# An attention and feed-forward kernel: a planner is told that one PSUM bank is one place

## The chip, the cores and the metric

The kernel runs on one core of a Trainium2 chip. The metric is the time of one execution on the device, in microseconds (us). Every time below is read from a timed run or from one profiled execution of the kernel before.

## What is computed

Attention with a threshold comes first, for 8 batches of 8 heads, 576 positions of width 64. Its output, laid out as 4608 tokens of 512, goes through a feed-forward layer of width 2048:

```python
scores = scale * np.matmul(q, k.transpose(0, 1, 3, 2))
thresh = np.max(scores, axis=-1, keepdims=True) - tau
scores = np.where(scores >= thresh, scores, -1000000000.0)
attn = softmax(scores)                  # written out with exp, sum and a 1e-9
x = np.matmul(attn, v)                  # 4608 tokens x 512 after a transpose
h = x @ w_in                            # 512 -> 2048
g = s * np.maximum(h, 0.0)**2 + b
out = g @ w_out                         # 2048 -> 512
```

## The kernel before

**Attention.** The work goes by visits: one visit is a pair of heads of one batch and half of its query rows. A visit has four or five tiles of 128 query rows by 576 keys. A tile's scores are made by TensorE into the PSUM tiles s0, s1 (early on also o): lines 352 and 341 in the early visits, line 363 (four matmuls, in split precision) and line 374 (the last 64 rows) later. VectorE takes the row's extreme (L395), ScalarE the exponential (L406), VectorE the threshold and sum (L409), GpSimd the division (L413). The weights are then transposed, in the first 8 visits by TensorE (L423, L425), later by VectorE and DMAs, and TensorE multiplies them by the values into the PSUM tile pv (L476).

**Feed-forward.** 256 tokens make a block, 18 blocks in all, and a block has 16 steps, one for each 128 columns of the inner width: 288 steps. A step is:
- its first products: 12 matmuls of 128x256 on TensorE (L599), into one half of the PSUM tile h. That tile is one bank of 512 columns, and even and odd steps take its two halves in turn (`k`, L590 and L593);
- its rectifier on ScalarE (L606), which reads that half, then a square (L607) and a rounded copy gh (L609), and a remainder gl on GpSimd (L610, in the last block on VectorE);
- its second products: twice three matmuls of 128x512 (L616), that take gh and gl as stationary operands and add to the PSUM tile o.

In the first and the last step of a block the first products are two pieces of six matmuls. Once, after the first block's steps, a matmul of line 563 writes the whole tile h.

**What sets the order.** Everything is recorded by `plan.add` with an engine, a cost, the function that emits it, a list of keys that it reads and one of keys that it writes, and a time `at` that serves as first rank. Keys are plain names: `plan.add` makes an operation depend on the last writer of what it reads, and on the last writer and all readers of what it writes. After that, `Plan.run` lays all operations out in time, many times over, forward and backward, under 18 settings, keeps the layout whose replay under four random delays is best by its own arithmetic, and emits the operations in that order. Each engine then runs its own instructions strictly in that order. The waits in the program do not come from the keys: the tile framework places them, from the tiles that the emitted instructions read and write and the order in which they were emitted. So the keys decide the order, and the order and the framework decide who waits.

Before the change, the keys of tile h are `h0` and `h1` for the halves, and `hs`, which only writers name. A step's first products write `h0` or `h1`, and `hs`; the rectifier reads `h0` or `h1` alone. Thus the plan keeps the first products of two steps in order, and lets a step's first products start while the rectifier of the step before is still to come. The early transposes of L425, which also use tile h in every other tile, write `h0` and `h1`.

Of the kernel before, what the change touches and what calls it, by code (L numbers as in the profile page):

```python
# [13 lines left out]
AF = mybir.ActivationFunctionType  # L14
# [160 lines left out]
def tile_attention_ffn(ctx: ExitStack, tc: tile.TileContext, qT, kT, v, tau, w_in, w_out, s, b, out):  # L175
    nc = tc.nc
# [55 lines left out]
    def pe(cost, fn, r, w, at):  # L232
        plan.add("PE", (cost, cost + 170), fn, r, w, at)
# [7 lines left out]
    def act(cost, fn, r, w, at):  # L241
        plan.add("ACT", cost, fn, r, w, at)
# [318 lines left out]

    def sums(at):
        pe(900, lambda: nc.tensor.matmul(bank["h"], ones.bitcast(F32), bias_t, start=True, stop=True), ["bias", "ones"],
           ["h0", "h1", "hs"], at)
        act((480, 620), lambda: nc.scalar.mul(out=bias_t, in_=bank["h"], mul=b_t), ["h0", "h1", "b"], ["bias"], at)

    def xhl():
        if "xhl" not in lazy:
            lazy["xhl"] = [sb(t, [P, NC, NB], F32R) for t in ("xh", "xl")]
        return lazy["xhl"]  # L570

    class Block:
# [16 lines left out]
        def step(self, f, at):  # L589
            k = count["step"] % 2  # L590
            count["step"] += 1
            n = (count["step"] - 1) % NG
            ps, g, hi, lo = bank["h"][:, k * NB:(k + 1) * NB], gb[k], gh[n], gl[n]  # L593

            def products(cs):
                xh, xl = xhl()
                for c in cs:
                    for i, (w, x) in enumerate(((wi[0][f], xh), (wi[0][f], xl), (wi[1][f], xh))):
                        nc.tensor.matmul(ps, w[:, c, :], x[:, c, :], start=(c == 0 and i == 0), stop=(c == NC - 1 and i == 2))  # L599
            if f in (0, NF - 1):  # L600
                for c in range(0, NC, 2):
                    pe(6 * 120.9, lambda c=c: products(range(c, c + 2)), [("xh", c // 2), ("xl", c // 2), (f"w{f}", "i")], [f"h{k}", "hs"], at)
            else:
                pe(3 * NC * 120.9, lambda: products(range(NC)), [(x, c) for x in ("xh", "xl") for c in range(2)] + [(f"w{f}", "i")],
                   [f"h{k}", "hs"], at)
            act((272, 383), lambda: nc.scalar.activation(out=g, in_=ps, func=AF.Relu), [f"h{k}"], [f"g{k}"], at)  # L606
            act((322, 417), lambda: nc.scalar.activation(out=g, in_=g, func=AF.Square), [f"g{k}"], [f"g{k}"], at)  # L607
            eng, do = (nc.vector, dve2) if self.last else (nc.gpsimd, pool)
            act((302, 405), lambda: nc.scalar.copy(out=hi, in_=g), [f"g{k}"], [f"gh{n}"], at)  # L609
            do((712, 740), lambda: eng.tensor_tensor(out=lo, in0=g, in1=hi.bitcast(F32), op=ALU.subtract),  # L610
               [f"g{k}", f"gh{n}"], [f"gl{n}"], at)

            def second(t):
                ts_ = slice(t * P, (t + 1) * P)
                for i, (a, w) in enumerate(((hi, wo[0][f]), (hi, wo[1][f]), (lo, wo[0][f]))):
                    nc.tensor.matmul(bank["o"][:, t, :], a[:, ts_], w, start=(f == 0 and i == 0),  # L616
                                     stop=(f == NF - 1 and i == 2))
            for t in range(2):
                pe(3 * 231.3, lambda t=t: second(t), [f"gh{n}", f"gl{n}", (f"w{f}", "o")],
                   [("o", t)] + (["o"] if f == 0 else []), at + SECOND)  # L620
# [115 lines left out]
    for f in range(FIRST_WEIGHTS):  # L736
        events.append((15 * f / FIRST_WEIGHTS, lambda f=f: convert(f)))
    step, when = 0, 0.0
    for i, (vs, j, t) in enumerate(tiles):
        joined = False  # L740
# [23 lines left out]
        for k_ in blocks:  # L764
            when = max(when, i + FFN_AFTER)
            each = 1.2 if i < 100 else 1.0

            def block(k_=k_, when=when, step=step, i=i, each=each):
                blk = make_block(*k_)
                blk.stage(max(i + FFN_AFTER, when - 1))  # L770
                for f in range(NF):
                    convert(f)
                    blk.step(f, when + each * f)
                    if not step and f == NF - 1:
                        sums(when + each * f + SUMS_AFTER)
                blk.finish(when + each * (NF + 1))

            events.append((i + (VALUES_AFTER if joins else 0) + 0.2, block))
            when += each * NF
            step += NF  # L780
# [47 lines left out]
```

## Time and profile before

| | us |
|---|---|
| timed runs, median of 3 | 1250.54 (1249.49 to 1253.12) |
| profiled execution, its own time | 1250.1 |
| profiled execution, first to last instruction | 1248.3 |
| TensorE busy in it | 1211.1 (97%) |
| ScalarE busy | 767.5 (61%) |
| VectorE busy | 807.1 (65%) |
| GpSimd busy | 719.7 (58%) |

Busy time is the union of an engine's instructions. TensorE's matmuls overlap one another in the records: one of 128x256 is shown for 0.28 us, and the next one starts 0.12 us after it, so idle time that the profile shows is a little less than what a pause really takes. In the rows, PE is TensorE, ACT ScalarE, DVE VectorE, POOL GpSimd, and L599 is line 599.

### The profile page before, as it was taken

To read this page: it belongs to the slowest core of one execution; us is meant where nothing else is said; L and a number is where in the kernel's file an instruction comes from. 1 tells how busy PE (TensorE), PEld (TensorE's weight loads), DVE (VectorE), ACT (ScalarE), POOL (GpSimd) and SP (SyncE) were. 2 spreads that over 40 slices of the span, in tenths; PEclk is the share of its full clock that TensorE was granted. 3 is DMA by queue.
4 is the path that set the end of the run, shared out by engine and by line. 5 is a ranking of instruction groups with operands and counts; after the bars stand their busy time and mean duration, and the time that the engine had idled before them with its cause. 6 is when DMAs were issued, how large, how long until landed. Compare 5 with 4: busy or idle time off the path is not lost.

```text
span 1248.3 us, 24523 instructions
## 1 busy us (share of the span) xinstructions
PE 1211.1 (97%) x7926; PEld 990.0 (79%) x7926; DVE 807.1 (65%) x2158; ACT 767.5 (61%) x1890; POOL 719.7 (58%) x822
## 2 busy tenths in 40 slices
PE   7789999999999999999999999999999999999998
PEld 5467778787887888788878888888888888887887
DVE  7987876667767676576666677666766666663011
ACT  5777755666666676565665666566656665653443
POOL 3766845576666775575565666557566656652200
PEclk7889999999999999999999999999999999999999
DMA  7950257678768776667666676566766666652000
GB/s 254 282 184 25 53 140 159 153 169 182 173 157 186 170 172 153 150 144 170 136 160 151 150 173 156 143 147 161 162 142 160 161 157 152 158 134 72 1 17 17
DMA packets 259534, 180.66 MB, mean 145 GB/s; under 512 B 83536, under 2 KB 238160, under 8 KB 259408
## 3 DMA queue, kind: packets, MB, share of 16 engines
q1 hardware_dynamic: 259120, 178.98, 59.0%
q8 instruction: 63, 1.03, 0.3%
q14 instruction: 63, 0.52, 0.1%
q10 hardware_dynamic: 288, 0.13, 0.0%
HBM read 87.03 MB, written 9.44 MB: 77 GB/s over the span
## 4 chain that ended last, share of the span: by engine, by line
PE 91%; DVE 4%; ACT 2%; issue 1%; DMA 1%; POOL 1%; SPq 0%; ACTq 0%; DVEq 0%; POOLq 0%
PE h L599 33%; PE o L616 32%; PE pv L476 12%; PE s L363 9%; PE s L352 2%; PE s L374 1%; DVE s L395 1%; ACT g L606 1%; PE pv L425 1%; DVE tr L409 1%; DMA qr<-in_q_dram 0%; DMA tau_t<-in_tau_dram 0%; DVE em L409 0%; DVE k L549 0%; PE o L352 0%
## 5 line engine op out<-in xcount | busy, mean ns | idle before, releaser
L599 PE MATMUL h<-xh,w 128*128 128x256 f32 x2304 | 466.7, 286 | 11.3 <-ACT g L606 11.0
L599 PEld LDWEIGHTS h<-xh,w 128*128 128x128 f32 x2304 | 376.9, 190 | 38.2 <-ACT g L606 23.5
L616 PE MATMUL o<-w,gh 128*128 128x512 f32 x1152 | 366.8, 400 | 0.8 <-DVE em L636 0.6
L599 PE MATMUL h<-xl,w 128*128 128x256 f32 x1152 | 326.1, 283 | 1.5 <-DVE xl L585 1.4
L610 POOL TENSOR_TENSOR gl<-g,gh 128x256 fp32r<-128x256 f32 x272 | 202.8, 747 | 212.0 <-ACT gh L609 188.2
L395 DVE TENSOR_SCALAR_CACHE_REDUCE s<-s,nsc 128x576 f32<-128x576 f32 x283 | 230.5, 819 | 143.1 <-PE s L363 120.8
L413 POOL TENSOR_SCALAR em<-em,st,zero 128x576 f32<-128x576 f32 x270 | 230.1, 853 | 156.7 <-DVE st L412 102.2
L409 DVE SCALAR_TENSOR_TENSOR em<-s,st,em 128x577 f32<-128x577 f32 x268 | 217.5, 812 | 105.8 <-ACT st L404 67.9
L406 ACT ACTIVATE em<-s,st 128x576 f32<-128x576 f32 x268 | 197.8, 738 | 95.9 <-DVE s L395 62.4
L616 PEld LDWEIGHTS o<-w,gh 128*128 128x128 f32 x1152 | 197.0, 189 | 46.3 <-issue 20.4
L616 PE MATMUL o<-w,gl 128*128 128x512 f32 x576 | 225.1, 391 | 0.0
L599 PEld LDWEIGHTS h<-xl,w 128*128 128x128 f32 x1152 | 219.7, 191 | 6.1 <-DVE xl L585 2.0
L446 DVE STREAM_TRANSPOSE tr<-em 128x512 f32<-128x512 f32 x252 | 178.2, 707 | 56.9 <-POOL em L413 47.3
L606 ACT ACTIVATE g<-h 128x256 f32<-128x256 f32 x288 | 109.2, 380 | 171.0 <-PE h L599 160.6
L328 POOL TENSOR_TENSOR k<-kr,k 64x576 fp32r<-64x576 f32 x104 | 148.5, 1428 | 54.1 <-ACT k L327 40.2
L476 PE MATMUL pv<-er,vb 128*64 128x256 f32 (+1 forms) x1280 | 172.8, 416 | 1.6 <-ACT er L434 1.6
L609 ACT CAST gh<-g 128x256 fp32r<-128x256 f32 x288 | 116.2, 405 | 56.6 <-PE o L616 52.9
L363 PE MATMUL s<-k 128*128 128x288 f32 x832 | 144.1, 297 | 0.6 <-POOL k L328 0.6
L363 PEld LDWEIGHTS s<-k 128*128 128x128 f32 x832 | 127.7, 188 | 19.7 <-issue 4.9
L476 PEld LDWEIGHTS pv<-er,vb 128*64 128x64 f32 x1280 | 86.4, 138 | 70.5 <-issue 12.9
L616 PEld LDWEIGHTS o<-w,gl 128*128 128x128 f32 x576 | 108.4, 188 | 24.5
L607 ACT ACTIVATE g<-g 128x256 f32<-128x256 f32 x288 | 119.9, 417 | 5.7
(104 smaller groups left out, 953.3 us busy)
## 6 DMA issues: line engine op xcount, KB each, us to landing
er<-tr SPq DMA_DIRECT2D x448, 160.0 KB, 3.3
kr<-in_k_dram SPq DMA_DIRECT2D x116, 288.0 KB, 4.2
vb<-in_v_dram SPq DMA_DIRECT2D x128, 128.0 KB, 2.8
qr<-in_q_dram SPq DMA_DIRECT2D x56, 160.0 KB, 4.4
er<-tr SPq DMA_DIRECT2D x112, 80.0 KB, 2.5
w<-in_moe_w_in_dram SPq DMA_DIRECT2D x16, 512.0 KB, 6.6
w<-in_moe_w_out_dram SPq DMA_DIRECT2D x16, 512.0 KB, 5.7
out_dram<-oo SPq DMA_DIRECT2D x30, 256.0 KB, 2.6
```

Source lines behind the costliest of these rows:

```text
L328: pool((1500, 1500), lambda: nc.gpsimd.tensor_tensor(out=z()[D:P], in0=kr[D:P, j], in1=z()[D:P].bitcast(F32), op=ALU.subtract), rk + [("z" ...
L363: nc.tensor.matmul(flat[sk][:, S0 + hf * HS:S0 + (hf + 1) * HS], lazy["q"][:, x, j, qc], lazy["k"][:, j, cs], start=(x == 0), stop=(x == 1))
L395: dve((740, 875), lambda: nc.vector.tensor_scalar(out=ps[:, S0:S0 + S], in0=ps[:, S0:S0 + S], scalar1=nsc, scalar2=None, op0=ALU.mult, op1 ...
L406: act((632, 740), lambda: nc.scalar.activation(out=ev, in_=ps[:, S0:S0 + S], func=AF.Exp, bias=st8[:, 0:1], scale=-1.0), [sk, (ks_, 0)], [ ...
L409: dve((742, 830), lambda: nc.vector.scalar_tensor_tensor(out=eb, in0=ps[:, S0:S0 + S + 1], scalar=st8[:, 1:2], in1=eb, op0=ALU.is_le, op1= ...
L413: pool((795, 825), lambda: nc.gpsimd.tensor_scalar(out=ev, in0=ev, scalar1=st8[:, 4:5], scalar2=zero, op0=ALU.mult, op1=ALU.add), [em_k, ( ...
L446: nc.vector.transpose(out=to[:, :, 0:NQ].rearrange("p m c q -> p m (c q)"), in_=ev[:, 0:M].rearrange("p (m r) -> p m r", m=4))
L476: nc.tensor.matmul(ps[j * D:(j + 1) * D, 0:32 * nb], vb[r, n, j, c], er[r, n, j, 0:nb, 32 * c:32 * c + 32], start=(c == 0), stop=(c == 4))
L599: nc.tensor.matmul(ps, w[:, c, :], x[:, c, :], start=(c == 0 and i == 0), stop=(c == NC - 1 and i == 2))
L606: act((272, 383), lambda: nc.scalar.activation(out=g, in_=ps, func=AF.Relu), [f"h{k}"], [f"g{k}"], at)
L610: do((712, 740), lambda: eng.tensor_tensor(out=lo, in0=g, in1=hi.bitcast(F32), op=ALU.subtract), [f"g{k}", f"gh{n}"], [f"gl{n}"], at)
L616: nc.tensor.matmul(bank["o"][:, t, :], a[:, ts_], w, start=(f == 0 and i == 0), stop=(f == NF - 1 and i == 2))
```

## The change

The key `hs` is dropped. First products and the matmul of L563 write `h0` and `h1` both, and the rectifier reads both. The plan therefore puts the first products of a step behind the rectifier of the step before. No instruction's work, shape or cost is altered; all of them are planned anew.

```diff
     def sums(at):
         pe(900, lambda: nc.tensor.matmul(bank["h"], ones.bitcast(F32), bias_t, start=True, stop=True), ["bias", "ones"],
-           ["h0", "h1", "hs"], at)
+           ["h0", "h1"], at)
...
                 for c in range(0, NC, 2):
-                    pe(6 * 120.9, lambda c=c: products(range(c, c + 2)), [("xh", c // 2), ("xl", c // 2), (f"w{f}", "i")], [f"h{k}", "hs"], at)
+                    pe(6 * 120.9, lambda c=c: products(range(c, c + 2)), [("xh", c // 2), ("xl", c // 2), (f"w{f}", "i")], ["h0", "h1"], at)
             else:
                 pe(3 * NC * 120.9, lambda: products(range(NC)), [(x, c) for x in ("xh", "xl") for c in range(2)] + [(f"w{f}", "i")],
-                   [f"h{k}", "hs"], at)
-            act((272, 383), lambda: nc.scalar.activation(out=g, in_=ps, func=AF.Relu), [f"h{k}"], [f"g{k}"], at)
+                   ["h0", "h1"], at)
+            act((272, 383), lambda: nc.scalar.activation(out=g, in_=ps, func=AF.Relu), ["h0", "h1"], [f"g{k}"], at)
```

The order moves nearly everywhere. Two places on TensorE and one on ScalarE follow. In the names, the number right after a w is the step within its block (w2 is step 2), xh and xl are the two parts of the tokens, gh and gl those of the step's result, and the last number is only the buffer's. What stands in brackets is whom an instruction waits for: Activation is ScalarE, Pool GpSimd.

TensorE before, eighth block, from the first products of step 2 to those of step 3:

```order
L599 MATMUL h_102<-xl_610,w2_359 128x256
L599 MATMUL h_102<-xh_609,w2_359 128x256
L599 MATMUL h_102<-xh_609,w3_427 128x256 [waits Activation_49]
L599 MATMUL h_102<-xl_610,w3_427 128x256
L599 MATMUL h_102<-xh_609,w3_427 128x256 x2
```

Step 3's products stand right behind step 2's, and their first matmul waits for ScalarE. TensorE after the change, the same place:

```order
L599 MATMUL h_102<-xl_597,w2_390 128x256
L599 MATMUL h_102<-xh_596,w2_390 128x256
L616 MATMUL o_100<-w15_1403,gh0_92 128x512 x2
L616 MATMUL o_100<-w15_1403,gl0_95 128x512
L363 MATMUL s0_98<-k_1514 128x288 [waits DVE_49,Pool_49]
L363 MATMUL s0_98<-k_1514 128x288 [waits Pool_49]
L363 MATMUL s0_98<-k_1514 128x288 x2
L599 MATMUL h_102<-xh_596,w3_440 128x256 [waits Activation_49]
L599 MATMUL h_102<-xl_597,w3_440 128x256
```

Three second products of the block before and the four score matmuls of a tile now stand between the two steps' products.

TensorE before, near the program's end, where attention is over: from the first products of step 1 of a block to those of step 2.

```order
L599 MATMUL h_102<-xl_610,w1_299 128x256
L599 MATMUL h_102<-xh_609,w1_299 128x256
L599 MATMUL h_102<-xh_609,w2_359 128x256 [waits Activation_49]
L599 MATMUL h_102<-xl_610,w2_359 128x256
L599 MATMUL h_102<-xh_609,w2_359 128x256 x2
```

Steps 1 and 2 adjoin here, and so do the products of steps 0 to 4 of this block. TensorE after, the same place:

```order
L599 MATMUL h_102<-xl_597,w1_297 128x256
L599 MATMUL h_102<-xh_596,w1_297 128x256
L616 MATMUL o_100<-w15_1403,gh0_92 128x512 [waits DVE_49]
L616 MATMUL o_100<-w15_1403,gh0_92 128x512
L616 MATMUL o_100<-w15_1403,gl0_95 128x512
L599 MATMUL h_102<-xh_596,w2_390 128x256 [waits Activation_49]
```

Three second products of the block before have come between; steps 2 and 3 still adjoin there.

ScalarE before, eighth block, the rectifiers of steps 0 to 2 (g0 and g1 are the two buffers that they write):

```order
L606 ACTIVATE g0_90<-h_102 128x256 [waits PE_49]
L607 ACTIVATE g0_90<-g0_90 128x256 [waits Activation_49]
L609 CAST gh1_93<-g0_90 128x256 [waits Activation_49]
L606 ACTIVATE g1_91<-h_102 128x256 [waits PE_49]
L406 ACTIVATE em0_77<-s0_98,st0_71 128x576 [waits DVE_49,Pool_49]
L607 ACTIVATE g1_91<-g1_91 128x256 [waits Activation_49]
L606 ACTIVATE g0_90<-h_102 128x256 [waits PE_49,Pool_49]
```

ScalarE after, the same place, the rectifiers of steps 0 and 1:

```order
L606 ACTIVATE g0_90<-h_102 128x256 [waits PE_49,Pool_49]
L404 ACTIVATE st4_75<-st4_75,tau8_67 128x1 [waits DVE_49]
L607 ACTIVATE g0_90<-g0_90 128x256 [waits Activation_49]
L406 ACTIVATE em0_77<-s0_98,st4_75 128x576 [waits Pool_49]
L609 CAST gh1_93<-g0_90 128x256 [waits PE_49,Activation_49]
L606 ACTIVATE g1_91<-h_102 128x256 [waits PE_49,Pool_49]
L607 ACTIVATE g1_91<-g1_91 128x256 [waits Activation_49]
L609 CAST gh2_94<-g1_91 128x256 [waits PE_49,Activation_49]
L406 ACTIVATE em1_78<-s1_99,st3_74 128x576 [waits DVE_49,Pool_49]
```

More of attention's work stands between the rectifiers than before, and an exponential can stand close ahead of one.

## Rows read from the trace of the kernel before

**Rows 1.** Page, busy time by engine, share of the span, instructions

```profile
PE 1211.1 (97%) x7926; PEld 990.0 (79%) x7926; DVE 807.1 (65%) x2158; ACT 767.5 (61%) x1890; POOL 719.7 (58%) x822
```

**Rows 2.** Page, the chain that ended last, by engine

```profile
PE 91%; DVE 4%; ACT 2%; issue 1%; DMA 1%; POOL 1%; SPq 0%; ACTq 0%; DVEq 0%; POOLq 0%
```

**Rows 3.** Stretches: length, busy (count) by engine, granted clock, DMA share, GB/s

```profile
0.00:70.00 70.00, 54.59 (x272) 34.48 (x272) 60.02 (x166) 46.28 (x93) 38.85 (x47) 0.80 0.83 262
70.00:160.00 90.00, 84.17 (x537) 63.52 (x538) 71.27 (x171) 65.30 (x163) 65.63 (x64) 0.98 0.27 78
...
300.00:500.00 200.00, 198.66 (x1351) 164.87 (x1352) 141.17 (x390) 130.91 (x324) 128.85 (x149) 1.00 0.74 170
...
1100.00:1150.00 50.00, 50.00 (x315) 39.46 (x314) 24.22 (x66) 25.30 (x64) 21.69 (x27) 1.00 0.43 101
1150.00:1248.30 98.30, 90.87 (x568) 80.64 (x567) 12.13 (x25) 39.26 (x98) 11.94 (x16) 0.99 0.06 17
```

**Rows 4.** TensorE's waits: who, for whom, us in total, times, longest

```profile
PE h L599 <- ACT g L606: 11.0, 21, 1.0
PE s L352 <- DVE em L409: 4.9, 3, 4.1
...
PE s L423 <- ACT er L432: 2.2, 1, 2.2
...
PE h L563 <- ACT g L606: 1.0, 1, 1.0
```

**Rows 5.** Time line of TensorE, eighth block: start, length, [idle before, releaser]

```profile
571.00 0.28 PE L599 MATMUL h<-xh,w 128*128 128x256 f32 x1
571.75 0.38 PE L599 MATMUL h<-xh,w 128*128 128x256 f32 x1 [0.47 <-ACT g L606]
571.97 0.28 PE L599 MATMUL h<-xl,w 128*128 128x256 f32 x1
572.09 0.40 PE L599 MATMUL h<-xh,w 128*128 128x256 f32 x2
```

**Rows 6.** Time line of ScalarE at the same place

```profile
568.66 0.68 ACT L327 CAST k<-kr 128x576 fp32r<-128x576 f32 x1 [0.23 <-DMA kr<-in_k_dram]
571.31 0.38 ACT L606 ACTIVATE g<-h 128x256 f32<-128x256 f32 x1 [1.98 <-PE h L599]
```

**Rows 7.** Time line of TensorE, first and last of 15 adjoining steps that paused

```profile
80.40 0.39 PE L599 MATMUL h<-xh,w 128*128 128x256 f32 x1 [0.47 <-ACT g L606]
1206.51 0.39 PE L599 MATMUL h<-xh,w 128*128 128x256 f32 x1 [0.47 <-ACT g L606]
```

**Rows 8.** Time line of TensorE, pauses at steps with other work between

```profile
118.38 0.39 PE L599 MATMUL h<-xh,w 128*128 128x256 f32 x1 [0.62 <-ACT g L606]
234.15 0.39 PE L599 MATMUL h<-xh,w 128*128 128x256 f32 x1 [0.54 <-ACT g L606]
302.92 0.39 PE L599 MATMUL h<-xh,w 128*128 128x256 f32 x1 [1.05 <-ACT g L606]
770.38 0.38 PE L599 MATMUL h<-xh,w 128*128 128x256 f32 x1 [0.16 <-ACT g L606]
901.47 0.39 PE L599 MATMUL h<-xh,w 128*128 128x256 f32 x1 [0.76 <-ACT g L606]
```

**Rows 9.** Time line of TensorE: second products, and scores, between two steps' products

```profile
575.44 0.70 PE L363 MATMUL s<-k 128*128 128x288 f32 x4
576.13 0.39 PE L599 MATMUL h<-xh,w 128*128 128x256 f32 x1
...
1226.21 0.63 PE L616 MATMUL o<-w,gh 128*128 128x512 f32 x2
1226.68 0.39 PE L616 MATMUL o<-w,gl 128*128 128x512 f32 x1
1226.91 0.62 PE L616 MATMUL o<-w,gh 128*128 128x512 f32 x2
...
1227.60 0.28 PE L599 MATMUL h<-xh,w 128*128 128x256 f32 x1
```

**Rows 10.** ScalarE's costliest lines: busy, mean ns, idle before and its releasers

```profile
L406 ACT ACTIVATE em<-s,st 128x576 f32<-128x576 f32 x268 | 197.8, 738 | 95.9 <-DVE s L395 62.4 <-DVE st L412 17.3 <-POOL gl L610 7.2
...
L606 ACT ACTIVATE g<-h 128x256 f32<-128x256 f32 x288 | 109.2, 380 | 171.0 <-PE h L599 160.6 <-POOL gl L610 6.6 <-POOL k L331 1.8
```

**Rows 11.** Stretch at the start, columns as in rows 3

```profile
10.00:20.00 10.00, 9.29 (x30) 5.78 (x31) 8.88 (x28) 5.83 (x12) 2.61 (x4) 0.55 0.96 329
```

## Prediction

> **What bounds the kernel now.** I read the page's busy times first. TensorE is busy 1211.1 of 1248.3 us, the next engine, VectorE, 807.1 [rows 1]. The chain of waits says the same: 91% of what ended last is TensorE's own work [rows 2]. So time can only be won where TensorE stands idle, 37.2 us in all, and the table by stretches tells where: 15.4 us in the first 70 us, 5.8 in the next 90, 1.3 in the 200 us from 300 to 500, none from 1100 to 1150, 7.4 in the last 98.3, most of which lies behind TensorE's last matmul [rows 3]. The list of waits names the causes. The largest by far is that first products (L599) wait for a rectifier (L606): 11.0 us in 21 pauses, and L563 waits once more for a rectifier, 1.0 us [rows 4]. Of the 21, 15 stand where a step's products follow the step before directly, each 0.47 to 0.53 us, 7.7 us in all, of which the first and the last are shown [rows 7]; the other six, 3.3 us, have other work between, and five of them are shown [rows 8].
>
> **How a pause at adjoining steps comes about.** The time lines at 571 us show it. The last product of a step starts at 571.00 and is shown for 0.28. ScalarE has been free since 569.34 (568.66 + 0.68), yet the rectifier starts only at 571.31, released by products [rows 6]; and it is the rectifier of the step before that, whose products had ended when this step's began. It waited for the other half of the bank to be written out. The next products start at 571.75 [rows 5], 0.06 after the rectifier's end. So in the program that runs, the two halves already exclude each other, and in the order in which they were emitted: where the plan emits a step's products before the last rectifier, that rectifier is held for a whole step, and the third step in a row pays the pause. The change takes no overlap away, since there is none; it tells the plan of a wait that is there anyway.
>
> A pause costs more than its idle time. From 571.97 to 572.09 one product follows the other after 0.12 us, though each is shown for 0.28 [rows 5]; so each pause costs its idle time and 0.16 more. At 571.75 that is 0.75 − 0.12 = 0.63; where the idle is 0.53 it is 0.69.
>
> **What the bank costs before.**
> - 15 pauses at adjoining steps: 7.7 + 15 × 0.16 = 10.1 us.
> - six with work between: 3.3 + 6 × 0.16 = 4.3.
> - L563: 1.0 + 0.16 = 1.2.
>
> Together 15.6 us, which is the most that the change can win here.
>
> **What it costs after.** I counted the 287 seams between the first products of neighbouring steps in both orders, and weighed the matmuls in each seam by start-to-start times: four score matmuls fill 576.13 − 575.44 − 0.16 = 0.53 us, six second products 1227.60 − 1226.21 = 1.39, so three fill 0.70 [rows 9]. Before, 63 seams put the products ahead of the last rectifier, 39 of them with nothing between; the other 224 are in the proper order, 17 of them with less than 0.8 us of work. After, all 287 are in the proper order; 2 have nothing between, 11 have under 0.8 us, 85 have 0.8 to 1.4, 189 more.
> - Two bare seams: at most 0.69 each, 1.4 us.
> - 11 short ones: the 17 of before had pauses of 0.54, 1.05, 0.16 and 0.76 [rows 8], with 4 × 0.16 that is 3.15, 0.185 per seam; so 2.0 us. (Bounds: 0, as at 13 of the 17, and 1.2 for each, 13 us.)
> - 274 with more: the 207 of before had two pauses, 0.62 [rows 8] and one that makes up the view's 11.0 with the rest, 0.16; with 0.32 that is 1.1, 0.005 per seam; so 1.5 us.
> - L563: in the new order three second products and four score matmuls stand between the step's last products and it: 0.
>
> Together 4.9 us; the gain is 15.6 − 4.9 = 10.7.
>
> What fills the seams is no new work, and it was somewhere before: does its cover now lack elsewhere? The second products of a step stand behind a chain of rectifier, square, copy and remainder. The nearest that they follow their first products in either order is 2.5 us of TensorE work at one place after and 4.2 before; in all other places it is over 4.1, as before. The score banks s0 and s1 are written again after as much work as before (4.1 us or more, at one place 3.4). ScalarE, GpSimd and VectorE have 35 to 42% to spare [rows 1]. I take 0 for this, within −1 and +2.
>
> **A rule that speaks against it.** At one seam, the rows show 0.75 us from the last product to the next one, the rectifier lying open in it [rows 5, 6]. The Trainium skill, Perfetto Trace Analysis, section Optimizing Tensor Performance (Matmuls), wants the opposite of one bank held in turn: independent groups of matmuls should rotate through PSUM banks, so that the emptying of one lies beside the next group's matmuls. By that rule alone, every seam would lie open, and the sum would be 287 × 0.69 = 198 us of loss in place of 4.9. The rows of before speak against it in this kernel: between two steps there is work for the banks o, s0, s1 and pv, and where 0.8 us or more of it stood there, 2 of 207 seams paused.
>
> **The start.** All operations are planned anew, the first 160 us too, where TensorE is idle 21.2 us [rows 3] and VectorE is busy 60.0 of 70. Ahead of the first products both orders have the same ten groups of scores, 17 groups of transposes and four value products; ahead of the eleventh step's, 15 groups of scores before and 16 after. I take 0. Bounds: the longest single waits there are 4.1 and 2.2 us [rows 4]; and the granted clock is 0.55 from 10 to 20 us [rows 11], close to the lower level (1.2 GHz, 0.5), so ten busy microseconds more or less of it are worth 4.5. Of these I take ±6 as the reach.
>
> **The sum.** The profiled execution took 1250.1 us, 1.8 more than its span. 1250.1 − 10.7 = 1239.4. The median of the timed runs is 0.4 above that execution, so 1239.8: I predict 1240.
>
> **The rivals.**
> 1. The start gives it back. If one more chain of 4.1 + 2.2 us lies open there and ten microseconds more fall to the lower clock, that is 6.3 + 4.5 = 10.8 against 10.7: 1250.6. For it: the start is where most idle time is, VectorE has no slack there, and this part of the plan moved as well. Against: the same work stands ahead of the first steps. Chance 0.16 (from +7 us on, it ends within 0.3%).
> 2. Slower: the rectifier is late. It runs in ScalarE's order, and behind an exponential of 0.74 us [rows 10] the least gap, 0.75 − 0.16 = 0.59 us, grows to 1.33; the 85 seams with 0.8 to 1.4 us between are then too thin. If they cost what the short ones do, 85 × 0.185 = 15.7 more, and the sum is 1239.8 + 15.7 = 1255.5. It turns the gain to nothing from 10.7 / 85 = 0.13 us a seam, and to slower from (10.7 + 3.8) / 85 = 0.17. For it: ScalarE is 61% busy, and there are more thin seams now. Against: of 45 such seams before none paused as long as the list of waits counts (0.15 us). Chance 0.06.
> 3. The skill's rule in full: 1239.8 + 193 = 1433, with all seams open. Chance 0.01.
> 4. The start wins too: 4 to 6 us of its idle time go along with the seams: 1235. Chance 0.07.
>
> **How the numbers follow.** The forecast has 0.70. About 0.3%, 3.8 us, is what a measurement of this kernel can tell from no change. Forecast and rival 4 are faster by more than that: 0.77. Rival 1 is the same: 0.16. Rivals 2 and 3 are slower: 0.07. The range: all of 15.6 won gives 1235, with a part of the start 1234; upwards it takes most of rival 1, up to 1248.
>
> **What would show it.** In the changed kernel's list of waits, L599 behind L606 should fall from 11.0 us in 21 pauses to 3 or 4 in under 10, and L563 should be gone. No adjoining pauses of 0.47 to 0.53 but at most two, late in the program. TensorE's idle time from 300 to 1150 us should be all but gone. ScalarE's idle time ahead of L606 (171.0 us [rows 10]) should fall, since no rectifier is held through another step's products. I am wrong if L599 still waits 8 us or more for L606, if pauses stand at seams with 0.8 to 1.4 us of work (rival 2), or if the idle time of the first 160 us moves by more than 6 from 21.2 (rivals 1 and 4).

## The result and the profile after

The changed kernel takes 1237.28 us, the median of 4 runs (1236.05 to 1237.95), against 1250.01 for the kernel before in the same runs: a ratio of 0.990, with a 95% interval of 0.987 to 0.992. Run again beside the experiments with pairs, it took 1237.42 (0.9888, 0.9865 to 0.9911). The forecast was 1240. The profiled execution took 1237.66 us and its span is 1235.7, 12.6 shorter.

TensorE's list of waits in the changed kernel (who, for whom, us in total, times, longest) begins thus:

```profile
PE s L352 <- DVE em L409: 3.6, 3, 2.7
PE s L423 <- ACT em L406: 3.0, 2, 2.3
PE pv L476 <- ACT er L434: 2.7, 3, 0.9
PE s L423 <- DVE s L395: 2.6, 1, 2.6
PE s L352 <- ACT er L432: 2.3, 1, 2.3
PE h L599 <- DVE xl L585: 2.0, 1, 2.0
...
PE h L599 <- ACT g L606: 1.0, 2, 0.5
```

First products waited 11.0 us in 21 pauses for a rectifier [rows 4]; now it is 1.0 in 2, and L563 is gone from the list. What leads it now is the early attention tiles' waits, of the first 160 us. The two pauses are at the two bare seams (nothing stands between two steps' products) of the new order:

```profile
1143.79 0.38 PE L599 MATMUL h<-xh,w 128*128 128x256 f32 x1 [0.53 <-ACT g L606]
...
1191.09 0.38 PE L599 MATMUL h<-xh,w 128*128 128x256 f32 x1 [0.47 <-ACT g L606]
```

How a filled seam looks, in TensorE's time line of the changed kernel, between two steps of the eighth block:

```profile
566.58 0.28 PE L599 MATMUL h<-xh,w 128*128 128x256 f32 x1
566.70 0.70 PE L363 MATMUL s<-k 128*128 128x288 f32 x4
567.23 0.63 PE L616 MATMUL o<-w,gh 128*128 128x512 f32 x2
567.70 0.39 PE L616 MATMUL o<-w,gl 128*128 128x512 f32 x1
567.93 0.28 PE L599 MATMUL h<-xh,w 128*128 128x256 f32 x1
```

and ScalarE beside it, the rectifier of the step that ended at 566.86:

```profile
566.96 0.38 ACT L606 ACTIVATE g<-h 128x256 f32<-128x256 f32 x1 [1.02 <-PE h L599]
```

It is done at 567.34, 0.6 us before the next products, and TensorE has no idle time in between. At the place of [rows 5] the rectifier came one step late and TensorE stood still for 0.47.

The stretches of the changed kernel (length, busy time and count by engine, granted clock, DMA share, GB/s):

```profile
0.00:70.00 70.00, 49.77 (x267) 31.33 (x267) 56.92 (x156) 45.08 (x90) 38.52 (x47) 0.85 0.77 252
70.00:160.00 90.00, 84.43 (x531) 63.88 (x529) 70.41 (x177) 65.56 (x162) 57.53 (x60) 0.94 0.29 85
...
300.00:500.00 200.00, 200.00 (x1359) 167.00 (x1359) 145.01 (x398) 131.17 (x328) 132.53 (x154) 1.00 0.74 172
```

Two things stand here beside [rows 3]. TensorE is idle 25.8 us of the first 160, where it was 21.2: 4.6 more. And from 300 to 500 us it is never idle, and 1359 matmuls run where it was 1351. The same view over 160 to 1150 us, of the kernel before and then of the changed one:

```profile
160.00:1150.00 990.00, 981.45 (x6554) 811.40 (x6553) 663.72 (x1799) 616.64 (x1538) 603.29 (x696) 1.00 0.66 155
```

```profile
160.00:1150.00 990.00, 988.02 (x6633) 822.80 (x6634) 661.76 (x1803) 621.91 (x1556) 608.22 (x704) 1.00 0.67 156
```

TensorE's busy time rises by 6.6 us, but 79 more matmuls run in the stretch, and at 990 / 6633 = 0.15 us each these are worth some 11.8, by an estimate that takes all matmuls for alike. The count in a fixed stretch shows what the idle time hides.

### The profile page after: what moved, and what is told of

The parts are those of the page before. It is cut to its first block, busy times and chain, and to the rows that moved or that the text cites. A ratio compares the mean times of both kernels' runs of the same rounds, so it can differ in the third digit from the quotient of the medians.

```text
span 1235.7 us, 24583 instructions
## 1 busy us (share of the span) xinstructions
PE 1202.7 (97%) x7926; PEld 989.8 (80%) x7926; DVE 800.5 (65%) x2158; ACT 766.2 (62%) x1890; POOL 713.1 (58%) x822
## 4 chain that ended last, share of the span: by engine, by line
PE 93%; DVE 3%; ACT 2%; issue 1%; DMA 1%; SPq 0%; POOL 0%; DVEq 0%; ACTq 0%; POOLq 0%
PE h L599 33%; PE o L616 33%; PE pv L476 13%; PE s L363 9%; PE s L352 2%; PE s L374 1%; DVE s L395 1%; PE pv L425 1%; DMA tau_t<-in_tau_dram 0%; PE s L341 0%; DMA er<-tr 0%; DVE tr L409 0%; PE s L423 0%; DVE em L409 0%; ACT em L406 0%
## 5 line engine op out<-in xcount | busy, mean ns | idle before, releaser
L599 PE MATMUL h<-xh,w 128*128 128x256 f32 x2304 | 469.3, 285 | 1.1 <-ACT g L606 1.0
L599 PEld LDWEIGHTS h<-xh,w 128*128 128x128 f32 x2304 | 378.8, 190 | 29.6 <-issue 8.5
L599 PE MATMUL h<-xl,w 128*128 128x256 f32 x1152 | 325.7, 283 | 2.0 <-DVE xl L585 2.0
L599 PEld LDWEIGHTS h<-xl,w 128*128 128x128 f32 x1152 | 219.5, 191 | 8.1 <-DVE xl L585 2.2
L606 ACT ACTIVATE g<-h 128x256 f32<-128x256 f32 x288 | 110.1, 382 | 183.9 <-PE h L599 167.4
```

## The experiments

The theory: the time is won at the seams, where a plan that knows of the bank's wait fills it. The first rival: any new plan moves the time by as much, and this one was lucky.

**Other settings of the planner, with the old keys and with the new.** `SHARES` and `LATER` are factors on the spare time that the planner adds to each operation, early in the program and later on. One of these lines differs, in two ways; each goes once with the keys of before and once with those of after.

```diff
-    SHARES = 0.2, 0.4, 0.7
+    SHARES = 0.25, 0.5, 0.8
```

```diff
-    LATER = 1.0, 1.2, 1.4
+    LATER = 1.1, 1.3, 1.5
```

> The keys of before, but the planner tries other settings (shares 0.25, 0.5, 0.8), so that everything is planned anew. In this order 43 seams between the first products of two steps have nothing between and 70 seams put the products ahead of the last rectifier (39 and 63 in the kernel before). Theory (the gain comes from the keys of the bank): 1250, within 4, with L599 waiting 9 to 14 us for L606. Rival (any new plan moves the time by 10 us or more, and this change was lucky): anywhere from 1235 to 1265, with no tie to the pauses at L599.

> The keys of after with the same other settings (shares 0.25, 0.5, 0.8). 4 seams with nothing between, none with the products ahead. Theory: 1238, within 4, at least 8 below its partner with the old keys; L599 waits under 4 us for L606. Rival (luck): it may lie anywhere, and not below its partner.

> The keys of before, a third set of settings (later 1.1, 1.3, 1.5). 43 bare seams, 69 with the products ahead. Theory: 1250, within 4, L599 waits 9 to 14 us for L606. Rival (luck): anywhere from 1235 to 1265.

> The keys of after with the third set of settings (later 1.1, 1.3, 1.5). 3 bare seams, none with the products ahead. Theory: 1238, within 4, at least 8 below its partner with the old keys; L599 waits under 4 us for L606. Rival (luck): not below its partner.

The ratios are to the kernel before as it ran beside each of them (medians 1250.01, 1251.28 for the pairs, 1248.96 for the wider search).

| kernel | median us | ratio to before | L599 waits for L606 | matmuls, 160 to 1150 us | TensorE idle, first 160 us | matmuls, first 160 us |
|---|---|---|---|---|---|---|
| before | 1250.01 | 1 | 11.0 us, 21 | 6554 | 21.2 | 809 |
| old keys, other shares | 1257.54 | 1.0059 (1.0039 to 1.0080) | 14.3, 29 | 6518 | 25.6 | 802 |
| old keys, other later | 1255.43 | 1.0035 (1.0017 to 1.0052) | 12.2, 24 | 6517 | 25.6 | 827 |
| after | 1237.28 | 0.9896 (0.9872 to 0.9920) | 1.0, 2 | 6633 | 25.8 | 795 |
| new keys, other shares | 1231.03 | 0.9844 (0.9814 to 0.9875) | 2.6, 5 | 6640 | 19.9 | 830 |
| new keys, other later | 1234.16 | 0.9868 (0.9843 to 0.9894) | 2.1, 5 | 6641 | 26.4 | 815 |
| wider search (below) | 1235.06 | 0.9887 (0.9860 to 0.9915) | 0.5, 1 | 6648 | 26.0 | 785 |

The pairs differ by 26.5 and 21.3 us, more than by 12.7. In the main part 6517 to 6554 matmuls run with the old keys and 6633 to 6648 with the new ones: in three plans against four the two groups lie far apart, so the keys decide that, not the plan's luck. The start goes by luck, as far as these plans show: 785 to 830 matmuls in the first 160 us, with no tie to the keys. Its idle time alone is a poor measure, since it also hangs on the granted clock. Two executions whose orders are the same in the start, of the changed kernel once more and of the one with bare pairs (both below), show it:

```profile
0.00:160.00 160.00, 133.97 (x795) 95.16 (x795) 127.25 (x332) 110.63 (x252) 96.12 (x106) 0.90 0.51 158
0.00:160.00 160.00, 137.93 (x798) 97.85 (x799) 128.00 (x334) 111.10 (x253) 94.77 (x107) 0.87 0.50 158
```

The second is idle 4.0 us less at a granted clock of 0.87 in place of 0.90, with only three matmuls more. By the counts, the kernel before had no lucky start among those of the old keys (809 beside 802 and 827); it was ahead of the other two in the main part, with 6554 matmuls and fewer pauses. The changed kernel, with 795, is the third of the four with the new keys. The forecast for the pairs missed on the size: the old keys came out 3.5 and 1.4 us above the range of 1246 to 1254, one of them with 14.3 us of waits where 9 to 14 were expected, and the new keys with other shares, at 1231.03, below 1234 to 1242; that is the best version found.

**The old order, with the rectifiers first.** The plan and its keys are those of before; only when operations are emitted, what a step's first products are put behind includes the last rectifier (and what that depends on).

```diff
-        return [ops[n][3] for _, n in self.order]
+        return [ops[n][3] for n in rectifiers_first(self)]
...
+def rectifiers_first(plan):
...
+        for d in sorted(plan.ops[n][4]) + [plan.ahead.get(n)]:
+            put(d)
```

> The plan of before, with its keys, but when the operations are emitted, each rectifier is put ahead of the next step's first products, with what it depends on. No rectifier is then held through another step's products, and the order of the matmuls stays nearly as it was: 30 seams have nothing between, 21 under 0.6 us. Theory (what costs is a seam that TensorE can't fill; the order on TensorE is what was won): 30 bare seams at 0.69 us are 20.7, against 10.1 before, and the short ones cost 3 to 5: slower than before by 5 to 12, 1255 to 1262, with L599 waiting 16 to 22 us for L606. Rival (what costs is the rectifier held in ScalarE's order, and what stands behind it): faster than before by 5 or more, 1245 or less.

Measured: 1286.2 us, 1.030 (1.027 to 1.032). The direction is the theory's and the rival is out, but the loss is 37 us where 5 to 12 were expected: L599 waits 39.2 us in 52 pauses. Of the 30 bare seams 27 pause for 0.47 to 0.53, as foretold. Of the other 22 pauses eleven take 1.49 to 1.88 us, most of these at seams that hold 1.39 us of second products. TensorE, ScalarE and GpSimd at one of them, in time lines of this kernel:

```profile
386.91 0.63 PE L616 MATMUL o<-w,gh 128*128 128x512 f32 x2
...
388.27 0.40 ACT L609 CAST gh<-g 128x256 fp32r<-128x256 f32 x1 [2.50 <-PE o L616]
388.76 0.72 POOL L610 TENSOR_TENSOR gl<-g,gh 128x256 fp32r<-128x256 f32 x1 [6.02 <-ACT gh L609]
...
389.51 0.38 ACT L606 ACTIVATE g<-h 128x256 f32<-128x256 f32 x1 [0.84 <-POOL gl L610]
...
389.95 0.39 PE L599 MATMUL h<-xh,w 128*128 128x256 f32 x1 [1.49 <-ACT g L606]
```

The rounded copy waits for a gh buffer, of which there are three, that second products have yet to read; GpSimd waits for the copy, the rectifier for GpSimd and its g buffer, and the next products for the rectifier. Where first products run ahead of second ones, the rectifier is at the end of that chain, and putting it first brings the whole chain in front of TensorE.

**Pairs with bare seams, and the same with held rectifiers.** These ask for the price of one seam with nothing else moved. Near the end of the changed kernel, 12 pairs of steps lose the second products between their first products, which follow behind the pair. In the second version the order on every engine is the same again, but the pair's first rectifier is emitted behind the pair.

```diff
+    for m in range(262, 286, 2):
...
+            if n in plan.second:
+                ahead[n] = last
```

```diff
+        rect = a + 1 + (plan.ops[a + 1][0] == "PE")
+        for n in range(b, last + 1):
+            plan.ops[n][4].discard(rect)
+        ahead[rect] = last
```

> The changed kernel once more, on the same chip as the two that follow. All theories: 1237, within 2.

> The changed kernel, but near the end, where attention is over, the first products of steps 262 and 263, 264 and 265, and so on to 284 and 285 are emitted without the second products between them, which follow behind the pair. Each rectifier still comes ahead of the next products. All matmuls stay, and the order on the other engines is the same; 13 seams are bare in place of 2. Theory (a bare seam costs 0.69 us on TensorE, a filled one nothing): 11 times 0.69 is 7.6, so 1244 to 1246, and L599 waits for L606 in 13 pauses or so, 6.5 us. Rival (the seams are not what the time hangs on, the plan as a whole is): 1237, within 2.

> The same order on every engine as in bare_pairs, but in each of the 12 pairs the first step's rectifier is emitted behind the second step's products, as the plan of before did it: TensorE need not wait inside a pair, and the rectifier is held until the second products of the bank are out. Theory (a held rectifier costs TensorE nothing as long as no third step follows at once; what costs is the wait for it): the 7.6 us go away again, 1237 to 1239. Rival (a rectifier that is held through another step's products costs time by itself, in ScalarE's order): 1242 or more.

Measured: 1237.42, 1245.95 (0.9967, 0.9955 to 0.9979) and 1237.15 (0.9897, 0.9877 to 0.9916), all three as the theory had them. With bare seams the kernel takes 8.5 us more, 0.78 for each of the 11; L599 waits 7.2 us in 14 pauses. One of the pairs, TensorE with bare seams:

```profile
1165.41 0.28 PE L599 MATMUL h<-xh,w 128*128 128x256 f32 x1
1166.22 0.38 PE L599 MATMUL h<-xh,w 128*128 128x256 f32 x1 [0.53 <-ACT g L606]
1166.44 0.28 PE L599 MATMUL h<-xl,w 128*128 128x256 f32 x1
```

From start to start that is 0.81 us in place of 0.12, and the second product, too, comes 0.22 after the first in place of 0.12. Together such a seam loses 0.79 us, and 0.73 where the idle time is 0.47. Six of the 11 new seams are of the first kind and five of the second: 8.4 us. Two other waits came with the new order. At a seam with three second products the next products wait 0.60 us, and elsewhere second products wait 0.84 us for VectorE:

```profile
1196.62 0.39 PE L599 MATMUL h<-xh,w 128*128 128x256 f32 x1 [0.60 <-ACT g L606]
1190.04 0.74 PE L616 MATMUL o<-w,gh 128*128 128x512 f32 x2 [0.84 <-DVE oo L636]
```

Single runs of the changed kernel lie up to 6 us apart here (1232.64 to 1238.43), so the 8.5 cannot be divided among these; the 8.4 is read from the rows. With held rectifiers, TensorE and then ScalarE at a pair of the same stretch:

```profile
1161.54 0.28 PE L599 MATMUL h<-xl,w 128*128 128x256 f32 x1
1161.66 0.40 PE L599 MATMUL h<-xh,w 128*128 128x256 f32 x2
```

```profile
1163.48 0.39 ACT L606 ACTIVATE g<-h 128x256 f32<-128x256 f32 x1 [2.70 <-PE h L599]
1164.94 0.38 ACT L606 ACTIVATE g<-h 128x256 f32<-128x256 f32 x1
```

The row of two at 1161.66 holds the last product of the first step and the first of the second: the products run on at 0.12 us; the first rectifier waits for both steps' products, with 2.70 us of idle time on ScalarE, and that costs nothing, since four groups of second products follow the pair. At one of the 12 pairs only three second products follow, and there the next step waits for the second rectifier (ScalarE, then TensorE):

```profile
1188.91 0.38 ACT L606 ACTIVATE g<-h 128x256 f32<-128x256 f32 x1
1189.34 0.38 PE L599 MATMUL h<-xh,w 128*128 128x256 f32 x1 [0.95 <-ACT g L606]
```

So a held rectifier is harmless where enough work follows, and a rectifier that TensorE must wait for is not. In the plan of before, the loss came where a third step followed, or where the seam was too thin.

**One more key of the same kind.**

```diff
-            pe(575, transposes, [em_k, "ident"], [kt] + kp, i + 0.5)
+            pe(575, transposes, [em_k, "ident"], [kt, sk] + kp, i + 0.5)
...
-                    out=e[0:T, NQ], in_=tt[:, c0:c1].rearrange("p (n q) -> p n q", n=nn)), [kt], ke, i + 0.5)
+                    out=e[0:T, NQ], in_=tt[:, c0:c1].rearrange("p (n q) -> p n q", n=nn)), [kt, sk], ke, i + 0.5)
```

> The keys of after, and one more of the same kind: the early transposes of L423 write columns of a score tile's bank under a key of their own; here they and the copy that reads them (L432) also hold that score tile's key. Only the first 8 visits, some 140 us, have such transposes. Theory (a plan that knows of the wait that is there loses less to it): L352 behind L432, 2.3 us, goes, and the idle time of TensorE in the first 160 us falls by 2 to 5 from 25.8: 1233 to 1236. Rival (the start is bound by VectorE's chain and the plan's luck): 1237, within 3.

Measured: 1286.73 us, 1.030 (1.028 to 1.033), 49 slower than the changed kernel, and both expectations are wrong. L352 behind L432 is indeed gone from this kernel's list of waits, but it begins:

```profile
PE s L423 <- POOL tr L413: 24.1, 8, 7.3
PE s L423 <- POOL em L413: 21.1, 8, 4.6
```

A key does more than tell of a wait: it fixes an order, the one in which operations were recorded. With it, the next tile's scores may no longer go into a bank before the last tile's weights have come through VectorE, ScalarE and GpSimd and are transposed. That work in advance was what hid this chain; in the first 160 us TensorE is now busy for 115.9, where it was 134.2, at a granted clock of 0.81 in place of 0.90. The last of these transposes now comes at 188 us in place of 148, and from 300 to 1150 us both kernels run 5712 matmuls: the loss lies ahead of that.

**A wider search.** The planner tries 60 settings.

```diff
-    SHARES = 0.2, 0.4, 0.7
-    LATER = 1.0, 1.2, 1.4
+    SHARES = 0.1, 0.25, 0.3, 0.5, 0.6, 0.8
+    LATER = 0.9, 1.0, 1.1, 1.2, 1.3
```

> The keys of after, and the planner tries 60 settings in place of 18 (shares 0.1, 0.25, 0.3, 0.5, 0.6, 0.8; later 0.9 to 1.3). One bare seam. Theory: the seams are nearly all filled already, so a better plan can only win in the first 160 us: 1234 to 1238. Rival (the new plan has more to give): under 1232.

Measured: 1235.06, as the theory had it. L599 waits once more for L606, near the end, and not at all from 160 to 1150 us. Its difference to 1231.03 is in the start, 785 matmuls in the first 160 us against 830; the wider search did not find that start.

## Why the prediction was right

**The mechanism held.** The bank already kept its halves apart, and the pauses at adjoining steps went with the steps' adjoining. With the old keys planned anew the pauses stayed, with the new keys they all but went (1.0 to 2.6 us in 2 to 5 waits), in each of three settings; and where the pairs brought bare seams back, the pauses and the time came back.

**Three terms of the sum were off, and that they nearly made up for each other is partly luck.**

- *The price of a pause was too small.* The sum put it at its idle time and 0.16. But the second product is late as well: 571.75 to 571.97 is 0.22 where 0.12 is usual [rows 5]. It is so behind each of the 21 pauses of before, 0.10 us each. A bare seam therefore loses 0.73 to 0.79 and not at most 0.69, which agrees with the 0.78 that the pairs measured.
- *The bank cost more before than 15.6, and less after than 4.9.* With the late second products, the 21 pauses come to 16.4 us from start to start, and L563 to 1.2. Further, at 17 seams the products start 0.05 us behind a rectifier's end with next to no idle time shown (under 0.4 us at all 17 together), since a pause of less than 0.16 us ends within the 0.28 for which the last matmul is shown; there another 4.0 us are lost. Together 21.6, so 15.6 was not "the most that the change can win". After the change, the two bare seams cost 1.5 and three seams of the other kind 0.6, together 2.1. Neither the 11 short nor the 274 other seams show a pause: the rate of 0.185 for a short seam, taken from four pauses in 17 seams of before, did not carry over. The bank thus gave 19.5, where 10.7 were forecast.
- *The start, taken as 0 within 6, lost more than it seems.* The idle time of its first 160 us rose by 4.6, but 2.1 of the idle time before were pauses of the bank (two of the 21, and L563), which went. Without them it rose from 19.1 to 25.8, by 6.7, at a granted clock of 0.90 in both kernels.

The span fell by 12.6. So 19.5 − 6.7 = 12.8 all but gives it. This is closer than the counting is: at seams where the rectifier has long ended, the second product is also 0.10 late behind some other work, 31 times before and 47 after, which would take off 1.6 more, and small differences elsewhere are not placed.

**The rivals.** Rival 1 (the start gives it back) happened in part, 4.6 of the 10.8 us in all, 6.7 beside the bank's own pauses. Rival 2 (a late rectifier at thin seams) did not: there are more seams with 0.8 to 1.4 us of work, and no pause at them. Rival 3, the rule of the Trainium skill, Perfetto Trace Analysis, section Optimizing Tensor Performance (Matmuls), that independent groups rotate through banks: the trace agrees with it where nothing else is there to run, and the pairs put the cost of leaving it at 0.78 us a seam. Where other banks have work, one bank held in turn showed no pause at 285 seams of the changed kernel. That needs enough work: with three second products between, one seam paused for 0.60 us with bare pairs and one for 0.95 with held rectifiers.

**Checks that were named.** L599 behind L606 was to fall to 3 or 4 us in under 10 pauses: 1.0 in 2. At most two pauses at adjoining steps, late in the program: so it is. TensorE's idle time from 300 to 1150 us was to be all but gone: it fell from 7.4 us to 1.1, and from 300 to 500 us from 1.3 [rows 3] to nothing. One check was wrong: ScalarE's idle time ahead of L606 was to fall from 171.0 [rows 10]; its row in the changed kernel is

```profile
L606 ACT ACTIVATE g<-h 128x256 f32<-128x256 f32 x288 | 110.1, 382 | 183.9 <-PE h L599 167.4 <-POOL gl L610 8.0 <-POOL k L328 4.8
```

ScalarE still waits for the products, more often and for shorter times (167.4 us in 168 waits, 3.0 the longest; before, 160.6 of [rows 10] in 141, 5.0 the longest). It has 38% to spare, and where its idle time stands says nothing here.

Either half of the edit is enough, by the order of the instructions: with the old keys for the products and both halves read by the rectifier, or the reverse, the plan comes out the same on every engine. Neither was run apart.

## What to carry to other kernels

Where a planner sets the order, its model of who excludes whom must match what the program will really wait for, but a key also fixes an order: add one where the fixed order still leaves the engine other work, and not where it forbids working ahead. Judge the change on the stage where it acts, and plan anew with several settings before believing a difference of 10 us in a kernel whose start is up to luck. In a pipelined engine, count instructions in a fixed stretch beside its idle time, and look at the granted clock of the stretch.

## What was not expected of the hardware

A rectifier held through another step's products costs no time that the runs can tell (1237.15 us against 1237.42), though ScalarE then idles 2.5 to 2.8 us at each of 12 places. The second matmul behind a pause came 0.10 us late as well, at each of the 21 pauses of before. And pauses too short to show idle time cost 4.0 us in the kernel before, at 17 seams, and 0.6 in the changed one.
